# One PSUM pool of bank pairs for scores and dense products, and a TensorE that keeps its array mode

## The chip, the cores and the metric

One core of one Trainium2 chip. The metric is the device time in microseconds of one execution, the median of several; a ratio is the mean time of one kernel's fast runs over that of the other's fast runs of the same rounds, so it is not quite the ratio of the medians quoted. The experiments ran in three batches with a median for the kernel before of 386.43, 385.22 and 385.07 us, so differences between batches of a microsecond or so mean nothing.

## The reference

Squared-ReLU attention over 8 batches of 12 heads (sequence 448, head dimension 64), then a feed-forward layer with a squared ReLU on its 3584 x 768 result:

```python
scores = scale * np.matmul(q, k.transpose(0, 1, 3, 2))      # (8, 12, 448, 448)
attn = np.maximum(scores, 0.0) ** 2 / S
x = np.matmul(attn, v)                                      # -> (3584, 768)
h = x @ w_in                                                # 768 x 2048
g = np.maximum(h, 0.0) ** 2
out = g @ w_out                                             # 2048 x 768
```

## The kernel before

The program contains a planner. It simulates the five engines, takes for each engine the ready operation with the earliest due time, hands out buffers, and so fixes the order in which instructions are issued; the tile framework then adds the waits. TensorE works in two ways: score and attention matmuls use the array as four tiles of 64x64 ("tile mode"), everything else uses it whole ("dense mode"). A score tile is two PSUM banks, written by four matmuls (a "round") and read out by one instruction over both banks. A dense product is one bank.

```python
SWITCH = {("dense", "tile"): 0.095, ("tile", "dense"): 0.115}   # the planner's cost of a mode change
...
"s": fixed(psum, "sp", 2, [P, 2, 512], FP32),      # two score tiles, a pair of banks each
"mm": fixed(psum, "mm", 4, [P, 512], FP32),        # four tiles of one bank for all else
...
def square(op, sp, width, pool="at"):              # read-out of a score tile, then its square
    first = plan.add([
        dve(n, lambda: nc.vector.tensor_scalar(
            out=rel(), in0=sp.tile[:, :, 0:width], scalar1=0.0, scalar2=SK,
            op0=ALU.max, op1=ALU.mult)),
        act(n, lambda: nc.scalar.activation(
            out=rel(), in_=sp.tile[:, :, 0:width], func=AF.Relu, scale=SK))], ...)
...
def evac_g(op, bank, b, fs, cols):                 # read-out of a product of the hidden layer
    one = plan.add([act(len(fs) * w, sq)], [op], [bank, g], ...)     # ACT squares out of the bank
    two = plan.add([dve(len(fs) * w, mask)], [one], [bank, g], ...)  # DVE masks by the bank's sign
...
for n, t in rs:                                    # two score rounds to a step
    op = scores([(n, t)], [sp], WHOLE, False)
    if chain is not None:
        chain.glue = op                            # keeps a step's tile work together
```

Of the kernel before, what the change touches and what calls it, by code (L numbers as in the profile page):

```python
# [42 lines left out]
class Plan:  # L43
# [2 lines left out]

    PATIENCE = 0.0, 0.15, 0.3, 0.45
    LEAD = 0.7, 0.9, 1.1, 1.3
    LAG = {"PE": 0.22, "ACT": 0.07, "DVE": 0.07, "POOL": 0.1, "SP": 0.0}
    SWITCH = {("dense", "tile"): 0.095, ("tile", "dense"): 0.115}  # L50

    def __init__(self, pools, busy):
        self.pools = {name: [(0.0, i, t) for i, t in enumerate(ts)] for name, ts in pools.items()}
        self.busy = busy
        self.sent: list = []
        self.ops: list = []
        self.now = 0.0
# [17 lines left out]
    def run(self):  # L75

        for z, op in enumerate(self.ops):
            op.id = z
        for op in reversed(self.ops):
            if not op.fixed or op.alts[0][0] != "PE":  # L80
                took = min(a[2] for a in op.alts)
                if len(op.alts[0]) > 4 and op.alts[0][4]:
                    took = 7.0
                due = min([x.due for x in op.nexts] or [1e6]) - took - 0.1
                op.due = due if op.due is None else min(op.due, due)
        start = {name: list(slots) for name, slots in self.pools.items()}, dict(self.busy)
        uses = [(b, b.left) for b in {b for op in self.ops for b in op.bufs}]

        def once(landing, rules):
            self.landing, (self.patience, self.lead) = dict(landing), rules  # L90
            self.pools = {name: list(slots) for name, slots in start[0].items()}
            self.busy, self.sent, self.order = dict(start[1]), [], []
            for b, left in uses:
                b.left, b.end, b.tile = left, 0.0, None
            self.simulate()
            return max(op.end for op in self.ops)

        best = None
        for rules in ((p, q) for p in self.PATIENCE for q in self.LEAD):
            landing: dict = {}  # L100
            for _ in range(6):
                try:
                    end = once(landing, rules)
                except RuntimeError:
                    break
                self.land()
                late = max(t - landing.get(z, 0.0) for z, t in self.landing.items())
                if late < 0.4 and (best is None or end < best[0]):
                    best = end, landing, rules
                landing = self.landing  # L110
        once(*best[1:])
        for emit in self.order:
            emit()
        return best[0]

    def land(self):


        queues: dict = {}
        for op in sorted((op for op in self.ops if op.size), key=lambda op: op.start):  # L120
            queues.setdefault(op.engine, deque()).append([op.start + 1.3, op.size, op])
        now, idle = 0.0, set(queues)
        while queues:
            for name in idle & set(queues):
                if queues[name][0][0] <= now + 1e-9 and set(queues) - idle:
                    queues[name][0][0] = now + 2.3
                    idle.discard(name)
            live = [name for name in queues if queues[name][0][0] <= now + 1e-9]
            idle -= set(live)
            if not live:  # L130
                now = min(q[0][0] for q in queues.values())
                continue
            rate = 400e3 / len(live)
            step = min(queues[name][0][1] / rate for name in live)
            later = [q[0][0] - now for q in queues.values() if q[0][0] > now + 1e-9]
            step = min([step] + later)
            now += step
            for name in live:
                q = queues[name]
                q[0][1] -= rate * step  # L140
                if q[0][1] <= 1e-3:
                    op = q.popleft()[2]
                    self.landing[op.id] = now + (
                        2.1 if len(queues) > 1 or now > 12.0 else 0.9) + (
                        0.6 if q and q[0][2].size > op.size else 0.0)
                    if not q or q[0][0] > now + 1e-9:
                        idle.add(name)
            queues = {name: q for name, q in queues.items() if q}

    def simulate(self):  # L150
# [10 lines left out]
        while done < len(self.ops):  # L161
# [6 lines left out]
            while again:  # L168
                again = False
                for eng in ("PE", "ACT", "DVE", "POOL", "SP"):  # L170
# [3 lines left out]
                    if eng == "PE" and last is not None and last.glue is not None:  # L174
# [4 lines left out]
                        if soon <= now:  # L179
                            got = waiting.index((last.glue.due, last.glue.id, last.glue)), (  # L180
                                last.glue.alts[0])
                    got = got or self.pick(eng, now, waiting)
                    if got is None:
                        if eng == "PE" and now < self.fill_until:
                            idle = now if idle is None else idle
                            if now < idle + self.patience:
                                heapq.heappush(events, idle + self.patience + 1e-3)
                            else:
                                self.fill(now)
                                heapq.heappush(events, self.busy[eng])  # L190
                        continue
# [17 lines left out]
                    if op.size:  # L209
                        op.end = max(begin + 2.2 + op.size / 390e3, self.landing.get(op.id, 0.0))  # L210
                        if eng == "POOL":
                            self.sent += [op.end + 0.8] * (2 if op.size == 458752 and took > 1.0 else 1)
                    if len(rest) > 1:
                        self.busy["POOL"] = max(self.busy["POOL"], self.busy[eng])
                    for b in op.bufs:
                        if b.tile is None:
                            slot = min(x for x in self.pools[b.pool] if x[0] <= now + 1e-9)
                            self.pools[b.pool].remove(slot)
                            b.tile, b.slot = slot[2], slot[1]
# [3 lines left out]
                    for b in op.bufs:  # L223
                        b.left -= 1
                        b.end = max(b.end, op.end + 0.07)
                        if not b.left:
                            self.pools[b.pool].append((b.end, b.slot, b.tile))
                            heapq.heappush(events, b.end)
                    for x in op.nexts:
                        x.wait -= 1  # L230
# [4 lines left out]
                    done += 1  # L235
                    again = True

    def soon(self, op):

        if op.wait or op.engine:  # L240
            return 1e9
        at, need = op.ready, {}
        for b in op.bufs:
            if b.tile is None:
                need[b.pool] = need.get(b.pool, 0) + 1
        for pool, k in need.items():
            slots = sorted(x[0] for x in self.pools[pool])
            at = max(at, slots[k - 1] if len(slots) >= k else 1e9)
        return at

    def fill(self, now):

        free = [x for x in self.pools["mm"] if x[0] <= now + 1e-9]
        if len(free) > 1:
            slot = min(free)
            self.order.append(lambda: self.filler(slot[2]))
            self.pools["mm"].remove(slot)
            self.pools["mm"].append((now + 0.2, slot[1], slot[2]))
        self.busy["PE"] = now + 0.11

    def pick(self, eng, now, waiting):
        for z, (_, _, op) in enumerate(waiting):
            if op.ready > now + 1e-9:
                continue
            for alt in op.alts:
                if alt[0] != eng:
# [9 lines left out]
                for b in op.bufs:  # L276
                    if b.tile is None:
                        need[b.pool] = need.get(b.pool, 0) + 1
                if all(sum(x[0] <= now + 1e-9 for x in self.pools[p]) >= k
                       for p, k in need.items()):  # L280
                    return z, alt
        return None
# [3 lines left out]
def kernel(  # L286
# [9 lines left out]
    nc = tc.nc  # L296
# [25 lines left out]
    def fixed(pool, name, n, shape, dt):  # L322
# [15 lines left out]
        "comb": fixed(sb, "comb", 6, [P, NH, P], FP16),  # L338
        "part": fixed(sb, "part", 6, [P, HALF], FP32),
        "rel": fixed(sb, "rel", 4, [P, 1024], FP32),  # L340
        "s": fixed(psum, "sp", 2, [P, 2, 512], FP32),
        "mm": fixed(psum, "mm", 4, [P, 512], FP32),
    }
    plan = Plan(pools, {"PE": 5.0, "ACT": 0.7, "DVE": 1.2, "POOL": 1.4, "SP": 0.7})
    plan.cold = 6.6

    def act(n, emit):
# [620 lines left out]
    PLAIN0 = True  # L968
    NPE = 6
    MERGE = True  # L970
    ROUNDS = NUN * TJ
    NB = ROUNDS // 2
    STREAM = NU * TJ
# [8 lines left out]
    nc.vector.memset(idle, 0.0)  # L982
    make_identity(nc, ident)
    for _ in range(9):
        nc.tensor.matmul(pools["mm"][3], lhsT=idle[:, 0:P], rhs=idle, start=True, stop=True)  # L985

    plan.fill_until = 45.0
    plan.filler = lambda bank: nc.tensor.matmul(  # L988
# [91 lines left out]
    for i in range(STREAM // 2, NB):  # L1080
# [19 lines left out]
        for n, t in rs:  # L1100
            sp = Buf("s")
            op = scores([(n, t)], [sp], WHOLE, False)
            todo.append((op, sp, n, t))
            if chain is not None:
                chain.glue = op
            chain = op
        for op, sp, n, t in todo:
            second, at = square(op, sp, S)
            ats[n, t] = second, at, lambda tl: tl
        if i in avs:  # L1110
            chain.glue = av(avs[i], list(range(TJ)))
            chain = chain.glue
        if i in pushes:
            push_dense(pushes[i])
        if i in avs and MERGE and i + 1 < NB:
# [43 lines left out]
```

## Time and profile before

| | before |
|---|---|
| time, median of the three runs before the prediction | 385.46 us |
| span of the profiled run | 383.4 us |
| TensorE busy | 374.7 us, 98% |
| DVE, ACT busy | 69%, 70% |
| TensorE idle from 45 us on, waiting for DVE | 0.6 us |
| visits to tile mode from 45 us on (counted in the timeline) | 57 |

A visit is a stretch of tile work between two stretches of dense work. The lines behind the table stand in the prediction below; PE is TensorE, PEld its weight loads, DVE is VectorE, ACT is ScalarE, POOL is GpSimd, and "<- X" names what ended an idle time.

### The profile page before, as it was taken

What the parts mean: (1) busy time and instruction counts of PE and PEld (TensorE: products, weight loads), DVE (VectorE), ACT (ScalarE), POOL (GpSimd) and SP (SyncE); (2) the same over time, 40 slices, a digit from 0 to 9 for tenths busy, and PEclk for the clock granted to TensorE, in tenths of its full rate; (3) what the DMA queues carried; (4) which work ended last, traced back from release to release, by engine and by line L of the source; (5) the groups of instructions that cost most, each with busy time, mean ns of one, the idle gap of its engine ahead of it and who ended that gap; (6) DMA issues with size and microseconds to landing.
All of it is one profiled execution on the core that took longest, in us unless ns stands there. A gap on an engine that the chain in (4) does not pass through costs nothing.

```text
span 383.4 us, 8363 instructions
## 1 busy us (share of the span) xinstructions
PE 374.7 (98%) x3311; PEld 200.4 (52%) x3311; DVE 266.2 (69%) x383; ACT 269.7 (70%) x407; POOL 194.5 (51%) x184
## 2 busy tenths in 40 slices
PE   8889999999999999999999999999999999999995
PEld 4545665444555445544555555544555546555563
DVE  2977789876785678676986575777784776256731
ACT  4998999797867886687786686697586785244221
POOL 7767747696735767565554474577413451001000
PEclk9999999999999999999999999999999999999999
DMA  9999999976668764868476566685562002200242
GB/s 184 170 207 202 190 229 246 245 172 155 85 168 191 178 157 86 171 161 211 71 172 147 140 133 131 177 169 146 87 124 52 2 3 61 63 21 3 57 109 82
DMA packets 70215, 51.34 MB, mean 134 GB/s; under 512 B 36896, under 2 KB 70176, under 8 KB 70176
## 3 DMA queue, kind: packets, MB, share of 16 engines
q1 hardware_dynamic: 52384, 35.86, 38.3%
q0 software_dynamic: 16928, 14.09, 24.7%
q10 hardware_dynamic: 864, 0.85, 0.6%
q8 instruction: 26, 0.43, 0.5%
q14 instruction: 13, 0.11, 0.1%
HBM read 45.61 MB, written 11.01 MB: 148 GB/s over the span
## 4 chain that ended last, share of the span: by engine, by line
PE 86%; DMA 5%; DVE 4%; ACT 2%; issue 1%; POOL 1%; DVEq 0%
PE mm L629 37%; PE mm L843 29%; PE sp L502 9%; PE mm L567 7%; DMA w<-in_moe_w_in_dram 5%; DVE comb L822 1%; DVE rel L529 1%; PE mm L985 1%; PE mm L441 1%; ACT at L536 1%; PE mm L778 1%; DVE wt L807 1%; POOL w L476 1%; PE mm L988 1%; ACT rel L532 0%
## 5 line engine op out<-in xcount | busy, mean ns | idle before, releaser
L629 PE MATMUL mm<-xt,w 128*128 128x448 f16 (+1 forms) x768 | 149.2, 346 | 0.0
L538 POOL TENSOR_TENSOR at<-rel 128x896 f16<-128x896 f32 (+1 forms) x63 | 102.4, 1627 | 91.4 <-ACT rel L532 63.7
L613 DVE SCALAR_TENSOR_TENSOR g<-mm,g 128x448 f16<-128x448 f32 (+1 forms) x128 | 76.5, 605 | 50.7 <-ACT g L618 50.5
L629 PEld LDWEIGHTS <-w 128*128 128x128 f16 x768 | 72.1, 98 | 70.3 <-issue 12.3
L529 DVE TENSOR_SCALAR rel<-sp 128x896 f32<-128x896 f32 (+3 forms) x87 | 90.7, 1046 | 23.0 <-PE sp L502 19.0
L618 ACT ACTIVATE g<-mm 128x448 f16<-128x448 f32 (+1 forms) x128 | 67.0, 529 | 45.0 <-PE mm L629 44.4
L536 ACT ACTIVATE at<-rel 128x896 f16<-128x896 f32 (+1 forms) x105 | 95.3, 925 | 4.7 <-PE mm L567 2.5
L532 ACT ACTIVATE rel<-sp 128x896 f32<-128x896 f32 (+1 forms) x87 | 77.5, 898 | 6.2 <-PE sp L502 5.1
L843 PEld LDWEIGHTS <-comb 128*128 128x128 f16 x416 | 39.9, 98 | 30.1 <-issue 3.5
L762 ACT ACTIVATE part<-mm 128x384 f32<-128x384 f32 x45 | 22.0, 488 | 44.0 <-PE mm L843 42.1
L502 PE MATMUL sp<-qkt,qkt 64*64 64x448 f16 (+2 forms) x756 | 51.0, 338 | 1.2 <-DVE rel L529 0.8
L421 POOL CAST blk<-raw 128x896 f16<-128x896 f32 x36 | 36.2, 1018 | 22.1 <-DMA raw<-in_k_dram 9.5
L855 DVE SCALAR_TENSOR_TENSOR part<-mm,part 128x384 f32<-128x384 f32 x52 | 28.5, 555 | 26.3 <-ACT part L762 14.9
L843 PE MATMUL mm<-wt,comb 128*128 128x384 f16 x208 | 37.0, 326 | 0.2 <-DVE comb L822 0.2
L843 PE MATMUL mm<-w,comb 128*128 128x384 f16 x208 | 36.8, 326 | 0.1
L567 PE MATMUL mm<-at,vs 64*64 64x448 f16 (+1 forms) x672 | 35.3, 343 | 0.0
L843 PEld LDWEIGHTS <-g 128*128 128x128 f16 x264 | 25.2, 98 | 19.0 <-issue 2.7
L502 PEld LDWEIGHTS <-qkt 64*64 64x64 f16 x756 | 18.1, 105 | 26.9 <-issue 23.4
L471 POOL DMA_DIRECT2D vs<-in_v_dram x48 | 29.9, 633 | 3.5 <-DMA w<-in_moe_w_in_dram 2.1
L744 POOL COPY rest<-g 128x1024 f16<-128x1024 f16 x8 | 9.9, 1239 | 41.6 <-DVE g L613 41.6
L843 PE MATMUL mm<-w,g 128*128 128x384 f16 x176 | 30.9, 326 | 0.0
L567 PEld LDWEIGHTS <-vs 64*64 64x64 f16 x756 | 22.5, 107 | 12.1 <-issue 2.2
(60 smaller groups left out, 217.1 us busy)
## 6 DMA issues: line engine op xcount, KB each, us to landing
out_dram<-part SPq DMA_DIRECT2D x108, 96.0 KB, 2.2
raw<-in_k_dram SPq DMA_DIRECT2D x18, 448.0 KB, 4.2
raw<-in_q_dram SPq DMA_DIRECT2D x18, 448.0 KB, 5.2
vs<-in_v_dram POOLq DMA_DIRECT2D x48, 112.0 KB, 4.5
w<-in_moe_w_in_dram POOLq DMA_DIRECT2D x4, 768.0 KB, 12.9
w<-in_moe_w_out_dram POOLq DMA_DIRECT2D x4, 768.0 KB, 13.5
g<-in_k_dram POOLq DMA_DIRECT2D x4, 224.0 KB, 11.4
g<-in_q_dram POOLq DMA_DIRECT2D x4, 224.0 KB, 10.1
```

The source lines that it names most:

```text
L421: return lambda: fn(blk.tile.rearrange("p t (f d) -> p f t d", f=2), tile_of().rearrange("p f (t d) -> p f t d", d=D))
L471: nc.gpsimd.dma_start(out=buf.tile[64 * r:64 * r + 64], in_=src[:, u, hs])
L502: nc.tensor.matmul(sp[64 * c:64 * c + 64, e, c0:c0 + w].rearrange("p (t c) -> p t c", c=TP), lhsT=kT[r, t, 64 * e:64 * e + 64], rhs=qT[r, ...
L529: dve(n, lambda: nc.vector.tensor_scalar(out=rel(), in0=sp.tile[:, :, 0:width], scalar1=0.0, scalar2=SK, op0=ALU.max, op1=ALU.mult)),
L532: act(n, lambda: nc.scalar.activation(out=rel(), in_=sp.tile[:, :, 0:width], func=AF.Relu, scale=SK))],
L536: act(n, lambda: nc.scalar.activation(out=dst(), in_=rel(), func=AF.Square)),
L538: lambda: nc.gpsimd.tensor_mul(dst(), rel(), rel()))],
L567: nc.tensor.matmul(banks[f].tile[64 * e:64 * e + 64, c0:c0 + w], lhsT=vs[r, e ^ c, t * D:(t + 1) * D], rhs=a[r, e, :], start=(t == 0), sto ...
L613: nc.vector.scalar_tensor_tensor(out=dst, in0=src, scalar=0.0, in1=dst, op0=ALU.is_gt, op1=ALU.mult)
L618: nc.scalar.activation(out=dst, in_=src, func=AF.Square)
L629: nc.tensor.matmul(bank.tile[:, c0:c0 + w], lhsT=w1[f // 4][:, m, f % 4 * P:(f % 4 + 1) * P], rhs=xts[b].tile[:, m, cols], start=(m == 0), ...
L843: nc.tensor.matmul(buf.tile[:, 0:HALF], lhsT=lhs()[:, j, :], rhs=w[:, j, :], start=(first and j == 0), stop=(j == NH - 1), skip_group_chec ...
```

## The change

Intent: scores should get up to four pairs when dense work leaves them free, and TensorE should change its mode less often (the "mode rule", `settle`). Two further lines change the planner's estimates of when a DMA has landed in the first 15 us ("landing estimates" below), and the glue is switched off. The diff's core (the planner's bookkeeping `free` and `give` and one call site of the glue are cut):

```diff
+    PSUM = "s", "mm"
+    WIDE, LATE, AHEAD = 3, 4.0, 4.0
+    steady = 45.0
...
-                        2.1 if len(queues) > 1 or now > 12.0 else 0.9) + (
+                        2.0 if now > 11.0 else 1.4 if len(queues) > 1 else 0.9) + (
...
+                    if eng == "PE" and got and now > self.steady:
+                        got = self.settle(got, mode, now, waiting)
...
-                            self.sent += [op.end + 0.8] * (...)
+                            self.sent += [op.end + (0.8 if op.end > 15.0 else 0.0)] * (...)
...
+    def take(self, b, now):
+        if b.pool == "s":
+            b.slot = min(range(len(self.psum)), key=lambda i: max(self.psum[i])), slice(0, 2)
+            b.tile = self.pairs[b.slot[0]]
+        else:                       # a dense product: a bank whose partner is in use comes first
+            i, h = min(((i, h) for i, x in enumerate(self.psum) for h in range(2)
+                        if x[h] <= now + 1e-9),
+                       key=lambda z: (self.psum[z[0]][1 - z[1]] <= now + 1e-9,
+                                      self.psum[z[0]][z[1]]))
+            b.slot = i, slice(h, h + 1)
+            b.tile = self.pairs[i][:, h, :]
...
+    def settle(self, got, mode, now, waiting):
+        other = waiting[got[0]][2]
+        if mode == other.mode or mode is None:
+            return got
+        if mode == "dense":
+            if "s" not in {b.pool for b in other.bufs if b.tile is None}:
+                room = self.WIDE
+            else:
+                room = sum(x <= now + 1e-9 for x in self.free("s"))
+            if room >= self.WIDE:
+                return got
+        ahead = self.LATE if mode == "dense" else self.AHEAD
+        same = self.pick("PE", now, waiting, mode)
+        if same and waiting[same[0]][2].due < other.due + ahead:
+            return same
+        return got
...
-        "s": fixed(psum, "sp", 2, [P, 2, 512], FP32),
-        "mm": fixed(psum, "mm", 4, [P, 512], FP32),
+    banks = fixed(psum, "ps", 4, [P, 2, 512], FP32)
...
+    GLUE = False
```

More of the change, by code (lines that the diff above doesn't have):

```diff
@@ L48, with __init__ @@
     LEAD = 0.7, 0.9, 1.1, 1.3
+    PSUM = "s", "mm"
+    WIDE, LATE, AHEAD = 3, 4.0, 4.0
+    steady = 45.0
     LAG = {"PE": 0.22, "ACT": 0.07, "DVE": 0.07, "POOL": 0.1, "SP": 0.0}
     SWITCH = {("dense", "tile"): 0.095, ("tile", "dense"): 0.115}
-    def __init__(self, pools, busy):
+    def __init__(self, pools, banks, busy):
+        self.pairs = banks
         self.pools = {name: [(0.0, i, t) for i, t in enumerate(ts)] for name, ts in pools.items()}
@@ L92, in once @@
             self.busy, self.sent, self.order = dict(start[1]), [], []
+            self.psum = [[0.0, 0.0] for _ in self.pairs]
             for b, left in uses:
@@ L211, in simulate @@
                         if eng == "POOL":
-                            self.sent += [op.end + 0.8] * (2 if op.size == 458752 and took > 1.0 else 1)
+                            self.sent += [op.end + (0.8 if op.end > 15.0 else 0.0)] * (2 if op.size == 458752 and took > 1.0 else 1)
                     if len(rest) > 1:
@@ L215, in simulate @@
                     for b in op.bufs:
-                        if b.tile is None:
+                        if b.tile is None and b.pool in self.PSUM:
+                            self.take(b, now)
+                        elif b.tile is None:
                             slot = min(x for x in self.pools[b.pool] if x[0] <= now + 1e-9)
@@ L226, in simulate @@
                         if not b.left:
-                            self.pools[b.pool].append((b.end, b.slot, b.tile))
+                            self.give(b)
                             heapq.heappush(events, b.end)
@@ L236, in simulate, with free, give @@
                     again = True
+    def free(self, pool):
+        if pool == "s":
+            return [max(x) for x in self.psum]
+        if pool == "mm":
+            return [t for x in self.psum for t in x]
+        return [x[0] for x in self.pools[pool]]
+    def take(self, b, now):
[9 more added lines that the diff above has]
+            b.tile = self.pairs[i][:, h, :]
+        i, hs = b.slot
+        self.psum[i][hs] = [1e9] * (hs.stop - hs.start)
+    def give(self, b):
+        if b.pool in self.PSUM:
+            i, hs = b.slot
+            self.psum[i][hs] = [b.end] * (hs.stop - hs.start)
+        else:
+            self.pools[b.pool].append((b.end, b.slot, b.tile))
     def soon(self, op):
@@ L246, in soon @@
         for pool, k in need.items():
-            slots = sorted(x[0] for x in self.pools[pool])
+            slots = sorted(self.free(pool))
             at = max(at, slots[k - 1] if len(slots) >= k else 1e9)
@@ L251, in fill, with pick @@
     def fill(self, now):
-        free = [x for x in self.pools["mm"] if x[0] <= now + 1e-9]
-        if len(free) > 1:
-            slot = min(free)
-            self.order.append(lambda: self.filler(slot[2]))
-            self.pools["mm"].remove(slot)
-            self.pools["mm"].append((now + 0.2, slot[1], slot[2]))
-        self.busy["PE"] = now + 0.11
-    def pick(self, eng, now, waiting):
+        if sum(x <= now + 1e-9 for x in self.free("mm")) > 1:
+            b = Buf("mm")
+            self.take(b, now)
+            self.order.append(lambda: self.filler(b.tile))
+            b.end = now + 0.2
+            self.give(b)
+        self.busy["PE"] = now + 0.11
+    def settle(self, got, mode, now, waiting):
[5 more added lines that the diff above has]
+                room = self.WIDE
+            else:
+                room = sum(x <= now + 1e-9 for x in self.free("s"))
[6 more added lines that the diff above has]
+        return got
+    def pick(self, eng, now, waiting, mode=None):
         for z, (_, _, op) in enumerate(waiting):
-            if op.ready > now + 1e-9:
+            if op.ready > now + 1e-9 or mode and mode != op.mode:
                 continue
@@ L278, in pick @@
                         need[b.pool] = need.get(b.pool, 0) + 1
-                if all(sum(x[0] <= now + 1e-9 for x in self.pools[p]) >= k
+                if all(sum(x <= now + 1e-9 for x in self.free(p)) >= k
                        for p, k in need.items()):
@@ L340 @@
         "rel": fixed(sb, "rel", 4, [P, 1024], FP32),
-        "s": fixed(psum, "sp", 2, [P, 2, 512], FP32),
-        "mm": fixed(psum, "mm", 4, [P, 512], FP32),
-    }
-    plan = Plan(pools, {"PE": 5.0, "ACT": 0.7, "DVE": 1.2, "POOL": 1.4, "SP": 0.7})
+    }
+    banks = fixed(psum, "ps", 4, [P, 2, 512], FP32)
+    plan = Plan(pools, banks, {"PE": 5.0, "ACT": 0.7, "DVE": 1.2, "POOL": 1.4, "SP": 0.7})
     plan.cold = 6.6
@@ L984 @@
     for _ in range(9):
-        nc.tensor.matmul(pools["mm"][3], lhsT=idle[:, 0:P], rhs=idle, start=True, stop=True)
+        nc.tensor.matmul(banks[3][:, 1, :], lhsT=idle[:, 0:P], rhs=idle, start=True, stop=True)
     plan.fill_until = 45.0
@@ L1103 @@
             todo.append((op, sp, n, t))
-            if chain is not None:
+            if chain is not None and GLUE:
                 chain.glue = op
@@ L1110 @@
         if i in avs:
-            chain.glue = av(avs[i], list(range(TJ)))
-            chain = chain.glue
+            last, chain = chain, av(avs[i], list(range(TJ)))
+            if GLUE:
+                last.glue = chain
         if i in pushes:
```

## The prediction

> **What bounds the kernel now.** I read the page's busy shares first, then the chain of work that ended last, then TensorE's waits, then its timeline, and last the DMA rate at the start. Busy shares and chain, from the page:
>
> ```profile
> PE 374.7 (98%) x3311; PEld 200.4 (52%) x3311; DVE 266.2 (69%) x383; ACT 269.7 (70%) x407; POOL 194.5 (51%) x184
> ...
> PE 86%; DMA 5%; DVE 4%; ACT 2%; issue 1%; POOL 1%; DVEq 0%
> ...
> L502 PEld LDWEIGHTS <-qkt 64*64 64x64 f16 x756 | 18.1, 105 | 26.9 <-issue 23.4
> ```
>
> TensorE (PE) is the bound: 98% busy, 86% of the chain. So only what shortens TensorE's own sequence, or lets it start earlier, can move the end. The third line shows what is still inside that 98%: the weight loads of the score matmuls (64x64 tiles) idled 26.9 us in total, and for 23.4 us of it they waited for nothing that a semaphore explains. The waits of the weight loads from 45 us on:
>
> ```profile
> PEld L502 <- issue: 20.1, 59, 0.7
> PEld L629 <- issue: 11.6, 35, 0.4
> PEld L843 <- issue: 6.9, 20, 0.4
> PEld L567 <- issue: 1.3, 4, 0.4
> PEld L778 <- issue: 1.1, 3, 0.4
> ```
>
> L502 (scores) and L567 (attention times v) use the array as 64x64 tiles; L629, L843 and L778 (dense products) use it whole. The unexplained gaps, about 0.34 us each, stand where the array goes from one mode to the other; on the way back there are 35+20+3 = 58. Walking the timeline from 45 us on I count 57 visits to tile mode: 33 of two score rounds, 18 of two rounds, an attention product and two rounds, 3 of one round, 3 of an attention product alone. Why two: the kernel has two score tiles in PSUM (a bank pair each), and four separate banks for the rest.
>
> The price of a visit, from the timeline and, for the pitch of undisturbed matmuls, from the chain:
>
> ```profile
> 131.91 3.58 PE L629 MATMUL mm<-xt,w 128*128 128x448 f16 x18
> 135.42 0.57 PE L502 MATMUL sp<-qkt,qkt 64*64 64x448 f16 x8
> 135.92 3.58 PE L629 MATMUL mm<-xt,w 128*128 128x448 f16 x18
> ```
>
> ```profile
> 125.69 5.78 PE mm L629 x30
> 131.97 3.51 PE mm L629 x18
> ...
> 140.00 1.32 PE mm L567 x28
> ```
>
> Pitch of a dense matmul: (5.78-3.51)/12 = 0.189 us. Four tile matmuls run at once; 28 of them, seven rounds, take 1.32, so 0.189 a round. From 131.91 to 135.92 is 4.01 us and holds 18 dense matmuls (3.40) and two rounds (0.38): 3.78. The rest, **0.23 us, is the price of a visit**. Another one (last dense start 146.52, second dense start of the next group 147.45, 384 columns at 0.1625) gives 0.235. Real waits of TensorE from 48 us on are two, 0.4 and 0.2 us. So the 57 visits cost 57 x 0.235 = **13.4 us**, 3.5% of the time, and nearly all else is work that the change leaves as it is.
>
> The start is another matter. Until 32 us the chain goes through the loads of w_in (its largest piece is 17.35 us long), and their issue is late. Windows of POOL at one microsecond each, last two columns DMA share and GB/s:
>
> ```profile
> 12.00:13.00 1.00, 1.00 (x3) 1.00 1.25 197
> 13.00:14.00 1.00, 1.00 (x2) 1.00 0.91 118
> 14.00:15.00 1.00, 1.00 (x2) 1.00 0.83 75
> 15.00:16.00 1.00, 1.00 (x2) 1.00 1.12 180
> ```
>
> At 197 GB/s the queue is full; between 13 and 16 us it lacks (79+122+17)/197 = 1.1 us of transfer. In POOL's timeline the last load of v is issued at 8.80, then POOL waits 1.47 us for a DVE result and squares until 12.06, and only then issues w_in.
>
> **What the Trainium skill says.** "TensorEngine Tiling (Array Packing)", Key Properties: "Mode switching requires drain", while tiles of one mode run independently. The trace agrees: four tile matmuls start 3 to 4 ns apart, and the mode change costs what I measured above (the page gives no figure). "TensorE: Matmul & The Clock Gate", Back-to-back issue gap: N/2.4 + 2.5 ns when warm, 189.2 for 448 columns; the trace has 189. So within a mode there is nothing left to save. "PSUM — Partial Sum Buffer", PSUM bank collisions: engines have to be kept apart per bank. So one bank of a pair can hold a dense product while the other is read out, and pooling is legal without new waits; the trace of before has no such pair to show it. The tiling page's PSUM Bottleneck section warns that read-out can become the limit once TensorE is faster; here ACT and DVE are at 70% and 69%, and between 48 and 328 us at 75% or so (42.9 and 39.0 us of the 48 from 48 to 96, 36.3 and 32.3 of those from 192 to 240).
>
> **The change part by part.** It adds and removes no instruction of the arithmetic; it alters the order in which a planner in the program issues it, and which bank each result takes.
>
> *Pooling.* Four bank pairs serve everything. Dense products prefer a bank whose partner is in use, so a steady dense stream sits in one pair (one bank filled, one or two read out) and three pairs are open to scores. Read-out of two score tiles is over 1.6 us after the visit begins (DVE rel 135.85+1.09, ACT rel 136.10+0.92, visit at 135.42); a third one I put at 2.5 to 3 us, as DVE has a mask of 0.61 in between. Dense groups of 1.13 to 1.3 us need a bank each meanwhile and find one. So three rounds every 4.6 us of dense work is sustainable.
>
> *Staying in mode.* From 45 us on, TensorE leaves dense mode for scores only with three free pairs, or when ready dense work lies over 4 us behind in order; in tile mode it takes tile work up to 4 us ahead. An attention product needs no score tile, so it is taken at once, and its 1.32 us let pairs come free for more scores behind it. Seven rounds and one attention product make a unit; before, 57 visits over 21 units are 2.7 each. After, I see per unit one visit with the attention product and four to five rounds, and two to three rounds left, which make two thirds of a visit to one visit of three: 1.7 to 2.0 visits a unit, so 35 to 42. I take 38. What speaks for fewer is attention visits with six rounds; for more, that two-stage dense products hold two accumulators for several microseconds each, so that often only two pairs are free and the 4 us run out. Saved: 19 x 0.235 = **4.5 us**, all of it on the path, since TensorE has no slack there.
>
> *No glue.* Scores of one step are no longer tied together; the mode rule takes its place. Worth nothing by itself.
>
> *Estimates of DMA landing at the start.* 1.4 in place of 2.1 us before 11 us, and no 0.8 us extra before 15 us in the count of DMAs under way, which had kept w_in from being issued. The planner can place w_in about 1.5 us earlier, ahead of the square at 10.86. At most the 1.1 us hole closes; as POOL still waits for real landings, I count **0.6 us**. It goes through to the end, because until 32 us the dense start waits for w_in (0.98 us of wait at 24.39) and after it TensorE is full.
>
> Sum: 4.5 + 0.6 = 5.1 us, so 385.5 - 5.1 = **380.4 us**.
>
> **Rivals.** (1) *Read-out takes the place of the switch.* Bursts of three to six rounds give ACT and DVE up to 6 x 0.95 us of first-stage work at once, and POOL or ACT the squares (1.63 or 0.93 us each); dense work then waits for a bank. For it: between 48 and 96 us ACT is at 89%. Against: before has almost no such wait, dense read-outs have earlier due times than pulled-ahead scores, and eight pooled banks hold no less than eight split ones. It would give back 1 to 3 us: 382 to 384. (2) *Blocks of attention results.* There are 11; an attention product frees seven at once, so scores pulled ahead of it wait with their squares. Then visits stay near 2.3 a unit, 48 in all, saving 2 us: about 383. (3) *It works better than I think*: 1.4 visits a unit, 30 in all, and the whole hole closed: 27 x 0.235 + 1.1 = 7.4 us, 378. Even that is short of 2% (377.75). (4) *The first 45 us get worse*, as scores may take four pairs and transposes wait for banks: plus 0.5 to 1 us.
>
> **Range and chances.** (3) sets the low end and (1) with (4) the high end: 377.3 to 383.5. Over 2% faster would need 33 visits fewer or a gain I don't see: 0.08. Over 2% slower would need a new wait of 13 us in a kernel that has under 1 us of such: 0.01. Within 2%: 0.91.
>
> **What would show it.** Visits to tile mode from 45 us on: 35 to 42, with three rounds in the common visit; the price of each still 0.23 us; gaps of PEld at L502 by "issue" down from 20.1 to 14 us or so; PE's busy time down by about 5 us and its share unchanged at 98%; w_in issued before 11 us and no dip in the DMA rate at 13 to 15 us. Wrong if visits stay above 48, if waits of TensorE's matmuls for DVE or ACT come to over 2 us after 45 us, or if the gain lies mostly before 45 us.

## The result, and the profile after

468.69 us (468.50 to 468.87) against 385.42: ratio 1.2159, 95% interval 1.2138 to 1.2180. Slower by 83 us, where 5 us of gain had been predicted.

The page's busy shares and its shares of the chain, kernel after:

```profile
PE 384.1 (82%) x3293; PEld 202.3 (43%) x3293; DVE 266.7 (57%) x387; ACT 277.4 (59%) x413; POOL 174.2 (37%) x174
...
PE 39%; DVE 11%; ACT 8%; issue 2%; DVEq 0%; ACTq 0%
```

The engines do the work of before (DVE 266.7 against 266.2, ACT 277.4 against 269.7), but TensorE is no longer full: 82% of a longer span. Of the 83.4 us by which the span grew, 74.0 are idle time of TensorE (82.7 against 8.7), and 9.4 are longer busy time on nearly the same matmuls (3293, and 3311 before). On the chain stand read-outs by DVE and ACT. (These shares sum to 60%: the chain could not be followed further back, so only its direction counts.) Who made TensorE wait, from 45 us on:

```profile
PE ps L686 <- DVE g L670: 19.9, 21, 1.6
PE ps L900 <- DVE part L912: 8.6, 10, 1.7
PE ps L686 <- ACT g L675: 5.4, 6, 1.2
PE ps L900 <- ACT part L819: 5.4, 9, 0.7
```

and before, all of them:

```profile
PE sp L502 <- DVE rel L529: 0.4, 1, 0.4
PE mm L843 <- DVE comb L822: 0.2, 1, 0.2
```

The columns are total us, times, longest us. In the trace TensorE's idle gaps from 45 us on sum to 67 us in some 95 gaps; before, to 0.7 us in 3. The weight loads, for comparison with the five lines in the prediction:

```profile
PEld L686 <- issue: 44.5, 65, 1.9
PEld L900 <- issue: 31.5, 52, 1.6
PEld L559 <- issue: 25.5, 59, 1.6
PEld L624 <- issue: 12.8, 18, 1.6
```

The gaps grew where no mode changes (L686, hidden layer: 44.5 us, the longest 1.9 where it had been 0.4). So this is not the cost of the mode change in another place.

The clearest stretch is at the end, where no score tile is in use any more and only dense products run. Chain of the kernel after, start and length in us:

```profile
405.44 2.44 PE ps L686 x12
407.88 0.02 issue
407.91 0.55 ACT g L675
408.46 0.02 issue
408.48 0.64 DVE g L670
409.12 0.02 issue
409.14 0.55 ACT g L675
409.70 0.02 issue
409.72 0.63 DVE g L670
410.35 0.04 issue
410.39 0.73 PE ps L686 x3
```

and ACT's timeline of the kernel before in the same kind of stretch:

```profile
336.85 0.54 ACT L618 ACTIVATE g<-mm 128x448 f16<-128x448 f32 x1 [0.59 <-PE mm L629]
337.98 0.54 ACT L618 ACTIVATE g<-mm 128x448 f16<-128x448 f32 x1 [0.59 <-PE mm L629]
339.12 0.54 ACT L618 ACTIVATE g<-mm 128x448 f16<-128x448 f32 x1 [0.59 <-PE mm L629]
```

Before, ACT reads out one product every 1.13 us, the time of a group of six matmuls, and TensorE never stops. After, the read-out of the first group starts only when twelve matmuls, two groups, are done. Then square, mask, square, mask follow one after the other, and only then does TensorE get its next bank: 4.95 us for three groups (405.44 to 410.39), of which 18 x 0.189 = 3.40 is work. In the program's listing the two groups of the twelve write the two halves of one pair, and the third group another pair. The waits in the programs say how. Call the first two groups A and B: the square of A waits for the last matmul of B, which goes into the other half; the square of B waits for the mask of A; and the next product into A's half waits for the mask of B. In the kernel before, no read-out waits for a matmul in a bank that it does not read (0 of 461 such waits); in the kernel after, 130 of 376 do.

### The profile page after: what moved, and what is told of

Read it like the earlier page. It is cut to its first block, busy times and chain, and to the rows that moved or that the text cites. A ratio compares the mean times of both kernels' runs of the same rounds, so it can differ in the third digit from the quotient of the medians.

```text
span 466.8 us, 8301 instructions
## 1 busy us (share of the span) xinstructions
PE 384.1 (82%) x3293; PEld 202.3 (43%) x3293; DVE 266.7 (57%) x387; ACT 277.4 (59%) x413; POOL 174.2 (37%) x174
## 4 chain that ended last, share of the span: by engine, by line
PE 39%; DVE 11%; ACT 8%; issue 2%; DVEq 0%; ACTq 0%
PE ps L900 19%; PE ps L686 17%; DVE g L670 5%; ACT g L675 5%; PE ps L624 3%; DVE part L912 3%; DVE comb L879 2%; ACT part L819 2%; PE ps L559 1%; DVE xt L646 1%; DVE rel L586 1%; DVE part L821 1%; ACT rel L589 1%; ACT at L593 0%; ACT xt L644 0%
## 5 line engine op out<-in xcount | busy, mean ns | idle before, releaser
L686 PE MATMUL ps<-xt,w 128*128 128x448 f16 (+1 forms) x768 | 150.6, 346 | 31.3 <-DVE g L670 19.9
L670 DVE SCALAR_TENSOR_TENSOR g<-ps,g 128x448 f16<-128x448 f32 (+1 forms) x128 | 75.9, 605 | 99.4 <-ACT g L675 81.3
L686 PEld LDWEIGHTS <-w 128*128 128x128 f16 x768 | 73.6, 97 | 104.1 <-issue 46.2
L675 ACT ACTIVATE g<-ps 128x448 f16<-128x448 f32 (+1 forms) x128 | 65.6, 529 | 85.0 <-PE ps L686 56.9
L586 DVE TENSOR_SCALAR rel<-ps 128x896 f32<-128x896 f32 (+3 forms) x89 | 92.2, 1046 | 13.2 <-PE ps L559 12.4
L589 ACT ACTIVATE rel<-ps 128x896 f32<-128x896 f32 (+1 forms) x85 | 74.1, 896 | 7.4 <-PE ps L559 6.6
L559 PE MATMUL ps<-qkt,qkt 64*64 64x448 f16 (+2 forms) x756 | 52.6, 342 | 8.5 <-DVE rel L586 3.2
L912 DVE SCALAR_TENSOR_TENSOR part<-ps,part 128x384 f32<-128x384 f32 x52 | 28.5, 554 | 42.2 <-PE ps L900 19.7
L900 PE MATMUL ps<-wt,comb 128*128 128x384 f16 x208 | 37.3, 326 | 8.2 <-DVE part L912 3.4
L624 PE MATMUL ps<-at,vs 64*64 64x448 f16 (+1 forms) x672 | 37.2, 345 | 7.2 <-ACT g L675 2.4
L900 PE MATMUL ps<-w,comb 128*128 128x384 f16 x208 | 37.1, 326 | 4.7 <-ACT part L819 3.6
L900 PE MATMUL ps<-w,g 128*128 128x384 f16 x176 | 31.4, 326 | 6.0 <-DVE part L912 1.9
```

The source lines that it names most:

```text
L559: nc.tensor.matmul(sp[64 * c:64 * c + 64, e, c0:c0 + w].rearrange("p (t c) -> p t c", c=TP), lhsT=kT[r, t, 64 * e:64 * e + 64], rhs=qT[r, ...
L586: dve(n, lambda: nc.vector.tensor_scalar(out=rel(), in0=sp.tile[:, :, 0:width], scalar1=0.0, scalar2=SK, op0=ALU.max, op1=ALU.mult)),
L589: act(n, lambda: nc.scalar.activation(out=rel(), in_=sp.tile[:, :, 0:width], func=AF.Relu, scale=SK))],
L624: nc.tensor.matmul(banks[f].tile[64 * e:64 * e + 64, c0:c0 + w], lhsT=vs[r, e ^ c, t * D:(t + 1) * D], rhs=a[r, e, :], start=(t == 0), sto ...
L670: nc.vector.scalar_tensor_tensor(out=dst, in0=src, scalar=0.0, in1=dst, op0=ALU.is_gt, op1=ALU.mult)
L675: nc.scalar.activation(out=dst, in_=src, func=AF.Square)
```

## The experiments

Two theories. **A**: the waits are made per PSUM tile. Before, a dense product's tile was a bank of its own; now it is half of a tile of two banks, so products and read-outs in the two halves order each other although they touch different banks. **B**: the mode rule's bursts of score rounds overload the read-out, and the tile is innocent. Eleven kernels ran, one of them twice, all with correct results.

### Same order, other tiles: halves_only

```diff
# from the kernel before
-        "mm": fixed(psum, "mm", 4, [P, 512], FP32),
+        "mm": [t[:, h, :] for t in fixed(psum, "mp", 2, [P, 2, 512], FP32) for h in range(2)],
```

I compared the two programs row by row: each engine issues the same instructions in the same order, on the same banks. Only where a tile ends differs, and with it the waits: 104 of 402 waits of a read-out for a matmul now name a bank that it does not read.

> The kernel before, with one change: its four dense banks are no longer four tiles of one bank but the two halves of two tiles of two banks. Every engine's instruction order is the same as before, as are the banks; only the waits that the framework derives can differ. Theory A (waits are derived per PSUM tile, so that a product in one half waits for the read-out of the other half): clearly slower, 395 to 450 us, with TensorE idle on DVE and ACT read-outs for more than 10 us after 45 us (before: 0.7 us). Theory B (the burst of score rounds under the mode rule overloads the read-out, the tiles do not matter): 385.4 us, within 0.3%.

447.55 us (446.49 to 448.06), ratio 1.1569 (1.1508 to 1.1631). That is theory A's upper end, and it comes without a mode rule, so theory B is not needed for a loss of this size. TensorE's waits from 45 us on:

```profile
PE mp L629 <- DVE g L613: 12.9, 25, 1.4
PE mp L567 <- DVE g L613: 5.5, 8, 0.9
PE sp L502 <- ACT rel L532: 5.1, 4, 1.4
PE mp L843 <- DVE part L855: 4.5, 4, 1.6
```

The second line is telling: an attention product (L567) waits for the mask of a hidden-layer product (g). In the program ten of the twelve such waits name a mask that reads the other bank of the tile. The tile boundary alone, with nothing else changed, costs 61 us against the 386.43 of its batch.

### A bigger dose: one_tile_for_four

```diff
# from the kernel before
-        "mm": fixed(psum, "mm", 4, [P, 512], FP32),
+        "mm": [t[:, 512 * h:512 * h + 512] for t in fixed(psum, "mp", 1, [P, 2048], FP32) for h in range(4)],
```

> The kernel before, its four dense banks now the quarters of one tile of four banks; instruction order and banks as before on every engine. Theory A (waits per tile) in a bigger dose: a read-out waits for the products issued before it and the next product for the read-out, so each of some 258 dense groups loses up to 1.1 us (a square of 0.53 and a mask of 0.61): 550 to 700 us, far above the 447.5 of two tiles of two. Rival (two particular banks side by side collide, whatever tile they are in): as the run with two tiles of two, 440 to 455 us.

698.07 us, ratio 1.8109. The loss grows with the number of banks in a tile, as A says (245 of 404 waits of a read-out for a matmul name another bank); two banks that happen to collide would have given 447 again. Part of it is not waiting: the mean granted clock of this run is 0.900 where the kernel before has 0.999, and between 600 and 640 us it is half:

```profile
600.00:640.00 40.00, 26.37 (x66) 0.50 0.00 0
```

(columns: window, length, TensorE busy and matmuls, granted clock, DMA share, GB/s). There one group of six takes 3.69 us, about 2.4 of it matmuls at the halved clock and 1.29 of waiting for the square and the mask. Between the profiled runs the span grew by 315 us: 234 are idle time of TensorE, and 81 are longer busy time with the slower clock.

### The parts of the change on the tiles as the change has them: pool_only

The kernel after with `steady` set beyond the end (no mode rule), the glue on, and the landing estimates of before.

> The changed kernel with pooled pairs, but without the mode rule, with the glue of before and the landing estimates of before. Theory A: most of the loss is here, 440 to 475 us. Theory B: near before, 383 to 390 us.

470.22 us, ratio 1.2161. Pooling alone has the whole loss; mode rule, missing glue and landing estimates together change it by less than 2 us.

### The mode rule alone: settle_only

The kernel after with the two score pairs and four dense banks of before as tiles of their own, `WIDE` 2, landing estimates of before.

> The kernel before with its split PSUM (two score pairs, four dense banks as tiles of their own), plus the mode rule alone (with two free score tiles as its threshold, no glue, landing estimates of before). Theory A: no loss, 383 to 387 us. Theory B (the mode rule and its bursts cost the time): above 420 us.

386.50 us, ratio 1.0004 (0.9960 to 1.0048). No loss from the rule, and no gain: 58 visits from 45 us on, where before has 57. As a test of B this is weak, since with two score pairs the bursts cannot grow; the next run is the strong one.

### The change on tiles of one bank: bank_tiles, and the same again

```diff
# from the kernel after
-    banks = fixed(psum, "ps", 4, [P, 2, 512], FP32)
+    ones = fixed(psum, "ps", 8, [P, 512], FP32)
+    banks = [ones[2 * i:2 * i + 2] for i in range(4)]
...
-            dve(n, lambda: nc.vector.tensor_scalar(
-                out=rel(), in0=sp.tile[:, :, 0:width], scalar1=0.0, scalar2=SK,
-                op0=ALU.max, op1=ALU.mult)),
+            ("DVE", 0.14 + 0.001045 * n, 0.22 + 0.001045 * n, lambda: [nc.vector.tensor_scalar(
+                out=rel()[:, e], in0=sp.tile[e][:, 0:width], scalar1=0.0, scalar2=SK,
+                op0=ALU.max, op1=ALU.mult) for e in range(2)]),
# the ACT way, the dense view and the score matmuls' views likewise
```

> The changed kernel with all of its rules, but eight PSUM tiles of one bank in place of four of two; a score tile is two of them, read out by two instructions of 448 columns in place of one of 896 (about 0.1 us more ACT or DVE time each). Theory A: the loss is gone, 381 to 390 us, TensorE idle after 45 us under 5 us. Theory B: the order of the mode rule is kept, so it stays slow, above 440 us.

384.62 us, ratio 0.9954 (0.9905 to 1.0003). The banks are pooled and the mode rule is on as in the kernel after, and the loss is gone: B falls here. No read-out waits for a matmul in another bank (0 of 622). TensorE's waits from 45 us on, all of them:

```profile
PE ps L560 <- DVE g L672: 0.7, 1, 0.7
PE ps L560 <- DVE rel L587: 0.5, 2, 0.3
PE ps L902 <- DVE comb L881: 0.3, 2, 0.2
```

> The bank-tile version of the changed kernel once more, with five rounds, as it is the only one so far that looked faster than before (ratio 0.9954, interval to 1.0003). If real: ratio 0.993 to 0.998 with an interval below 1. If noise: 1.000.

384.14 us, ratio 0.9964 (0.9933 to 0.9995). A gain of 0.4%. Both runs of this version come out below the kernel before, but only the second one's interval stays below 1.

### Pooling alone on tiles of one bank: bank_pool_only

bank_tiles without the mode rule, with the glue and the landing estimates of before: the counterpart of pool_only.

> Pooling alone with eight tiles of one bank (no mode rule, glue and landing estimates of before): the counterpart of the pool-only run that took 470 us. Theory A: 384 to 389 us. If pooling is bad for another reason (dense work and scores taking banks from each other): above 400 us.

390.50 us, ratio 1.0136 (1.0106 to 1.0165), slightly above the expected band. Against pool_only's 470.22, the tiles are worth 80 us. In the profiled run the granted clock was 0.50 between 16 and 20 us, so its start is not typical; the one run at clock 1.00 took 389.09, so the clock can hold about 1.4 us of the median.

### Control of the split read-out: split_read

The kernel before, its two score pairs made of tiles of one bank and read out in two instructions, as in bank_tiles.

> Control: the kernel before with its split pools, but each score tile two tiles of one bank, read out by two instructions of 448 columns. If the split read-out itself is hidden (theory of the bank-tile run): 384.5 to 387 us. If it costs what its added ACT and DVE time suggests (some 0.1 us times 174 read-outs, on engines at 70%), a rival to the mode rule as the reason for the small gain there: 388 us or more.

390.68 us, ratio 1.0149 (1.0116 to 1.0182): the rival's side. But the profiled run (span 387.8) has one wait of 2.7 us of a dense product for a sum on DVE, which bank_tiles, with the same split, lacks; bank_pool_only, at 390.5, has one of 2.7 us too. The planner makes a new order for each duration that it is told, so the cost of the split itself and the luck of the order can't be told apart here.

### The landing estimates: landing_only and bank_tiles_old_landing

The first is the kernel before with the two lines of landing estimates changed, the second bank_tiles with those two lines as before.

> The kernel before with the changed estimates of DMA landing alone. By the prediction's term: the load of w_in goes out about a microsecond earlier, the dip in DMA rate at 13 to 15 us closes, 0.6 us gained: 384.0 to 385.2 us. Rival: the order that the planner then finds differs elsewhere by more than that; anything from 384 to 389 us, with the dip closed all the same.

386.13 us, ratio 1.0006 (0.9967 to 1.0045). The load of w_in goes out at 11.40 in place of 12.06. The dip is half closed (140, 144 and 184 GB/s at 13 to 16 us, so 0.6 us lacking at 197 in place of 1.1). To see where time is won, add up the matmuls issued by 45 us, each at its pitch (0.189 us for 448 columns, in proportion for fewer, a quarter of it on a 64x64 tile; fillers, whose results are not used, left out): 28.5 us of work, where the kernel before has 28.2. So 0.3 us is won at the start, but nothing arrives at the end: other waits (1.4 us for a sum on DVE, 1.2 us for a score read-out) stand in this order.

> The bank-tile version with the landing estimates of before, mode rule kept: between the pooling-only bank-tile run (390.5) and the full one (384.6). If the mode rule makes their difference: near 385. If the landing estimates make it: near 390.

390.47 us, ratio 1.0127 (1.0088 to 1.0166). So on tiles of one bank the difference between 390.5 and 384.4 goes with the landing estimates and not with the mode rule, though the same two lines are worth nothing on the kernel before. It does not come from earlier loads: by 45 us this run has 27.6 us of matmul work done and bank_tiles 27.7; by 100 us it is 76.4 against 78.5, by 300 us 264.1 against 269.4. Of the 6 us, some 3.5 are TensorE's idle gaps from 45 us on (5.0 us in 12 gaps against 1.5 in 5), most of them for one sum on DVE, where bank_tiles waits 0.3:

```profile
PE ps L902 <- DVE comb L881: 2.9, 3, 1.8
```

So what the two lines changed here is the order that the planner found later on. Why this order has the waits stays open.

### The price of a visit: merge_off, and fewer visits: bank_tiles_eager

merge_off is the kernel before with `MERGE = False`: the step after an attention product is no longer put next to it.

> The kernel before with one flag turned: the step after an attention product is no longer merged with it, so the program has 87 stretches of tile work in place of 74. If a visit costs 0.235 us, as predicted from the trace: 13 x 0.235 = 3.1 us more, 388 to 389 us. If visits are free because something else bounds: 385.5 us.

390.11 us, ratio 1.0120 (1.0093 to 1.0146). From 45 us on there are 70 visits, 13 more. PEld's waits for nothing, to be held against the lines in the prediction:

```profile
PEld L502 <- issue: 24.4, 72, 0.5
PEld L629 <- issue: 13.3, 38, 0.4
PEld L843 <- issue: 9.7, 28, 0.4
```

The span is 5.1 us longer. Of it, 1.3 us are lost before 45 us (49 dense matmuls are behind it there, against 59 before; the granted clock was 0.96 there, against 1.00), so 3.8 us stand against the predicted 13 x 0.235 = 3.1. The price was about right, as far as one re-planned order can tell.

bank_tiles_eager is bank_tiles with `WIDE, LATE, AHEAD = 2, 4.0, 8.0`.

> The bank-tile version with other constants of the mode rule (two free pairs suffice, 8 us of look-ahead in tile mode): 60 stretches of tile work in the whole program in place of 65. By the visit price: 5 x 0.235 = 1.2 us less than the bank-tile version, 383 to 384 us. If the longer bursts cost read-out waits: equal or slower, 385 to 388 us.

384.85 us, ratio 0.9986 (0.9949 to 1.0024). 48 visits against 51 or 52, but 3.1 us of idle gaps from 45 us on against 1.5. By these numbers three or four fewer visits save some 0.8 us and the gaps give 1.6 back; on the clock the two versions can't be told apart.

## Why the prediction was wrong

**The step that failed** is the one on pooling: "So one bank of a pair can hold a dense product while the other is read out, and pooling is legal without new waits". I took the statement of "PSUM — Partial Sum Buffer", PSUM bank collisions, on when engines collide, per bank, for a statement on which waits the program gets. I noted that the trace of before had no such pair to show it, and counted the waits as zero all the same. halves_only measures the term: 61 us for the tile boundary alone, in an unchanged order. In the changed kernel it is about 84 us, the difference between 468.7 and bank_tiles' 384.6, which has the same pool, rules and estimates on tiles of one bank. The changed order makes it worse than in halves_only, I think because `take` puts a dense product into the pair whose other half is in use, which I had read as a virtue: three pairs stay open. It is exactly the placement in which a product meets a read-out. That share is argued from the code and the end of the trace; no run changes the preference alone. Two of the prediction's own signs of being wrong came true: waits of TensorE far over 2 us after 45 us, and visits above 48.

**What bounds the kernel** was right for before. After, as the stretch at the end shows, the bound moved from TensorE's work to the round trip of product, square and mask within a pair.

**The visits** were misjudged apart from that: 35 to 42 predicted, 55 counted in the changed kernel, 51 or 52 in bank_tiles. Three rounds did become the commonest visit (18 of 55), but 15 of two rounds remain, and the attention visits hold mostly two to four rounds of scores, not four to five. Of the mode rule's 4.5 us there is no trace: settle_only 1.0004, and bank_tiles_old_landing (390.5) equals bank_pool_only (390.5). Nor does the rule lower the count: bank_pool_only, without it, has 51 visits too.

**The price of a visit**, 0.235 us, held up: 3.8 us measured for 13 visits where 3.1 were expected, with an uncertain correction for the start. (The prediction's second reading, from 146.52 to 147.45, gives 0.23 and not 0.235; 57 visits are then 13.1 us in place of 13.4.)

**The landing estimates**: the mechanism was half right. In the changed kernel the load of w_in went out at 11.10 us in place of 12.06, and the windows at 13 to 16 us show 193, 174 and 188 GB/s where there had been 118, 75 and 180. But landing_only shows 0.3 us of the 0.6 at 45 us and nothing at the end, while on tiles of one bank the two lines go with 6 us that arise long after the loads have landed. A re-planned kernel seems to move by some microseconds through its order alone; a term of 0.6 us is below that.

**The rivals**: (1), read-out in the place of the switch, named the right place on the chain but the wrong reason: a lack of read-out speed, worth 1 to 3 us. DVE and ACT are less busy after (57% and 59%) than before. What is scarce is not their time but the permission to start. (2), visits near 48, was the closest on visits (51 or 52 on tiles of one bank), but the 2 us that it left as a gain did not come. (4), a worse first 45 us, came true and was too small: the changed kernel has 23.8 us of matmul work done by then, the kernel before 28.2, so 4.4 us are lost in place of 0.5 to 1; on tiles of one bank it is 0.5 or less. The range did not follow from the rivals either: (1) at 384 with 1 us of (4) is 385, not 383.5.

**The chances**: 0.01 for a loss over 2%, on the ground that no wait of 13 us was in sight. A wait that the trace of before cannot show, because the kernel before has no such sharing, should not have been given that little.

## What to carry to other kernels

When a change cuts buffers out of a larger tile, ask first at which grain the waits are made, and test it by moving nothing but the tile boundary: same order, same banks, one line of edit. Idle time that ends with a release by a group that shares only the tile, and read-outs that start after two groups where they used to start after one, are its marks in a profile. If several small tiles must also be read as one, weigh the second instruction (here 1.5% in split_read, the luck of the order included) against the sharing (16% in halves_only).

## What the Trainium skill lacked or had wrong

- "PSUM — Partial Sum Buffer", PSUM bank collisions: it gives the bank (and quadrant) as the unit in which engines have to be kept apart, and advises to guard by bank. That is right as a condition, but it does not warn that the waits a program gets can be coarser. With tiles of two banks they were made per tile: 447.6 us against 386.4 in the same instruction order, and 698.1 with four banks in one tile. No page that I read has it.
- "TensorEngine Tiling (Array Packing)", Key Properties: it says that a change of tiling mode drains TensorE, without a figure. Here a visit to 64x64 tiles and back cost 0.23 us in the trace of before, and 13 added visits some 3.8 us.
- "TensorE: Matmul & The Clock Gate", Why this matters for your kernels: it asks for no idle gaps above about 3 us between bursts. In the four-bank run the granted clock was 0.50 from 600 to 640 us with gaps of only 1.29 us, one in each 3.69 us, while in the changed kernel five gaps of 1.39 us, one in each 4.95 us, went with a clock of 1.00 (384 to 432 us). So between these two runs it was not the length of the gap that decided; the same page's second failure mode (micro-idles while PSUM banks are cycled) fits that better, but gives no share of idle time at which it begins.
